# The last six token tiles as three units of 1024 tokens, the first FFN product by Strassen's seven products, with weight sums built on the chip and streamed back from DRAM

## The chip, the cores and the metric

The kernel runs on one core of one Trainium2 chip. The metric is the time of one execution in microseconds of device time; a run's figure is the median of several executions. The program is written in Bass with a hand-written order: the text of the program is the order of instructions on each engine. TensorE (PE) multiplies, VectorE (DVE), ScalarE (ACT) and GpSimd (POOL) work elementwise, and SyncE (SP) issues the transfers.

## What is computed

The reference, cut to what matters. Attention is local: each block of 64 tokens attends only to itself.

```python
def _attn_ref(q, k, v):                       # B, H, S, D = 8, 8, 576, 64
    ...
    scores = scale * np.matmul(q_c, k_c.transpose(0, 1, 2, 4, 3))     # chunks of 64
    scores = scores - np.max(scores, axis=-1, keepdims=True)
    attn = np.exp(scores)
    attn = attn / (np.sum(attn, axis=-1, keepdims=True) + 1e-09)
    out = np.matmul(attn, v_c)
    ...
def _moe_ref(x, g_ln, w_ch1, w_ch2):          # 4608 tokens, 512 -> 2048 -> 512
    ...
    xn = (x - mu) / np.sqrt(var + 1e-06) * g_ln
    ch = np.maximum(xn @ w_ch1, 0.0) @ w_ch2
    return (x + ch).astype(np.float32)
```

## The kernel before, in words

The 4608 tokens are 9 tiles of 512 (`NTILE`), each tile two pairs of 256 (`PAIR`, 18 pairs). Every matmul operand of the FFN is held as a high and a low part, and a product is the sum of three matmuls: high by high, high by low, low by high. The hidden width 2048 is cut into 16 slices `f` of 128.

Per tile, `ffn` runs over the 16 slices. `up(f)` (L427) makes the hidden slice `h`, 128 by 512 tokens, in one PSUM bank: 4 slices of the width 512 by 3 terms, 12 matmuls at L437. `split(f)` rectifies it on ACT into the high part `hh` (L447) and leaves the remainder `hl` on DVE (L448). `down(f)` (L453) adds 12 matmuls (4 token blocks by 3 terms, L458) into the four PSUM banks `y`. `finish` (L471) scales `y` by the reciprocal root of the variance, adds `x` and stores. So a tile has 192 matmuls of 128x512 in the first product and 192 in the second. PSUM has 8 banks: 2 for attention (`ps_a`), 2 for `h` (`ps_h`), 4 for `y` (`ps_y`).

`attention` is a generator; each `next` on it issues one step for one pair: loads; scores (L243, 64 small matmuls); row maxima `top`; subtraction and exponential; 16 transposes of 32x256 on DVE (L298); row sums; the product with V into two `ps_h` banks (L327); scaling to `x`; statistics (L371); `xg` (L376); 16 more transposes of 32x256 on DVE (L410) and the split into `xth` (ACT, L415) and `xtl` (POOL, L416). With `by_pe` the transposes are done on TensorE instead, into `ps_a` banks, and copied out by ACT.

All weights stay in SBUF as `wp[f]` once they are converted from the float64 words that come from DRAM (`convert_w`). The strings `START`, `STEADY` and `LAST` are the order: each letter advances one generator (`u` the FFN matmuls, `1` split or finish, capital letters attention). `START` covers tile 0 and the weight conversion. `STEADY` is played for tiles 1 to 7 and carries two pairs of attention for the tiles behind; `LAST` is tile 8 alone. SP issues every transfer but a few in program order; an issue that waits for something holds those behind it.

Of the kernel before, what the change touches and what calls it, by code (L numbers as in the profile page):

```python
# [8 lines left out]
F32 = mybir.dt.float32  # L9
# [8 lines left out]
P = 128  # L18
# [16 lines left out]
START = "kkwkwakwbkwkwkawwwwaawwbwabbkwAkwawbwakkabkkaabaAbabauw1Abbub1Bkbwvuuwuw12wwAvvvw22AwvwvuAvw2wwAvvw1u2AuwwBwvuv12vBuuwyywABA1ww3Ayww3wAywAyuwwwwA3y3BywBBBwBEyyBBwy3w3yywBwwyww3BwwyByy3ywy33yy3E"  # L35
STEADY = "ABu1Au1AuAu1AuAu1AuABuAu1AEu1AuAu1AuAu1AuAu1BuBu1BuBu1BuBu1BuBEuBBu1BBu1BuBBu1Buu1uu1"
LAST = "u1u1uu1uu1uu1uu1uu1uu1uu1uu1uu1uu1uu1uu1uu1uu1u1"

# [7 lines left out]

ROOM = (3, 11)

F64_LOW = float.fromhex("0x1p-15")
F64_HIGH = float.fromhex("0x1.dffffep+16")  # L50


# [5 lines left out]
def chunk_attention_ffn(ctx: ExitStack, tc: tile.TileContext, qkv, v01, g, w, out):  # L58
# [12 lines left out]
    ps_h = ctx.enter_context(tc.tile_pool(name="ps_h", bufs=2, space=PSUM))  # L71
    ps_y = ctx.enter_context(tc.tile_pool(name="ps_y", bufs=4, space=PSUM))

    ident = const.tile([P, P], F32, name="ident")
# [130 lines left out]

    def attention(pair, xt_cols, xs, by_pe, den_by_pe):

# [161 lines left out]
        for j in range(2):  # L369
            stats = small.tile([P, nc.vector.BN_STATS_DIM], F32, name="stats")  # L370
            nc.vector.bn_stats(out=stats, in_=x[:, j, :])  # L371
            nc.vector.bn_aggr(out=mv[:, j, :], in_=stats)
        yield
        xg = work.tile([P, 2, DM], F32, name="xg", tag="work")
        for j in range(2):
            nc.vector.scalar_tensor_tensor(  # L376
                out=xg[:, j, :], in0=x[:, j, :], scalar=mv[:, j, 0:1], in1=g_sb, op0=ALU.subtract, op1=ALU.mult
            )
        yield

        xth, xtl = xt_cols()
# [38 lines left out]
    def ffn(pairs, xt, xs, f0, f1, room=()):  # L420
# [3 lines left out]
        hs, held = {}, []  # L424
        tail = pairs[-1] == 2 * NTILE - 1

# [16 lines left out]
        def split(f):  # L443
            if slots == 1 or not held:
                held[:] = [hp_.tile([P, slots, nt], F32R, name=f"h{i}") for i in "hl"]
            h, (hh, hl) = hs[f], (x[:, f % slots, :] for x in held)
            nc.scalar.activation(hh, h, AF.Relu)  # L447
            nc.vector.scalar_tensor_tensor(  # L448
                out=hl, in0=h, scalar=0.0, in1=hh.bitcast(F32), op0=ALU.max, op1=ALU.subtract
            )  # L450
            hs[f] = hh, hl
# [19 lines left out]
        def finish(j):  # L471
            pair, jj = pairs[j // 2], j % 2
            x, rstd = xs[pair]
            nc.vector.scalar_tensor_tensor(  # L474
                out=x[:, jj, :], in0=sums(pair)[jj], scalar=rstd[:, jj : jj + 1], in1=x[:, jj, :],
# [31 lines left out]
        def rectified():  # L507
            for f in range(f0, f1):
                assert f < f0 + 2 or f - 2 in done
                split(f)  # L510
# [9 lines left out]

        return products(), rectified()

    def play(order, streams):
        for c in order:
            next(streams[c])
# [3 lines left out]
    class Tokens:  # L529
# [10 lines left out]
        def attention(self, i, by_pe=False, den_by_pe=False):  # L540
            return attention(2 * self.t + i, lambda: self.cols(i), xs, by_pe, den_by_pe)

# [13 lines left out]
    with tc.manual_schedule():  # L556
        nc.scalar.activation(minus, ident, AF.Copy, scale=-1.0)
        play(START, now)
        for t in range(1, NTILE):
            now.update(zip("u1", tiles[t].ffn(0, 2, room=ROOM if t + 1 < NTILE else ())))  # L560
            if t + 1 < NTILE:
                now.update(A=now.pop("E"), B=tiles[t + 1].attention(1))
            now["E"] = tiles[t + 2].attention(0) if t + 2 < NTILE else iter("  ")
            play(STEADY if t + 1 < NTILE else LAST, now)

# [34 lines left out]
```

## Time and profile before

| what | value |
|---|---|
| time, median of 3 runs | 864.1 us (863.63 to 864.87) |
| span of the profiled execution, first to last instruction | 862.8 us |
| tile 1 starts on PE | 131.7 us |
| one period of two tiles in `STEADY` | 183.1 us (247.57 to 430.66) |
| bytes moved in the whole execution | 60.39 MB, mean 70 GB/s |

The profile is one execution taken by the hardware profiler; the median of the timed runs lies 1.3 us above its span. A matmul's listed duration contains the pipeline; how far apart matmuls start is what counts for a full PE. The busy share of an engine is a mean over stages that have different limits, so the stages are read one by one.

### The profile page before, as it was taken

What the parts mean: (1) busy time and instruction counts of PE and PEld (TensorE: products, weight loads), DVE (VectorE), ACT (ScalarE), POOL (GpSimd) and SP (SyncE); (2) the same over time, 40 slices, a digit from 0 to 9 for tenths busy, and PEclk for the clock granted to TensorE, in tenths of its full rate; (3) what the DMA queues carried; (4) which work ended last, traced back from release to release, by engine and by line L of the source; (5) the groups of instructions that cost most, each with busy time, mean ns of one, the idle gap of its engine ahead of it and who ended that gap; (6) DMA issues with size and microseconds to landing.
All of it is one profiled execution on the core that took longest, in us unless ns stands there. A gap on an engine that the chain in (4) does not pass through costs nothing.

```text
span 862.8 us, 13752 instructions
## 1 busy us (share of the span) xinstructions
PE 852.4 (99%) x5946; PEld 704.5 (82%) x5946; DVE 526.1 (61%) x960; ACT 178.6 (21%) x267; POOL 56.7 (7%) x64
## 2 busy tenths in 40 slices
PE   7999999999999999999999999999999999999998
PEld 5888888888888888888888888888888888888886
DVE  6989957567556665666657575676566656661112
ACT  5766431021112121201111111211120212011110
POOL 0110000010101010101000100101010101010000
PEclk9999999999999999999999999999999999999999
DMA  9996503200320032001310032003200300010001
GB/s 356 331 291 182 195 1 123 74 1 2 122 74 1 1 111 86 1 1 39 112 47 2 1 122 74 1 2 122 75 1 2 121 27 1 1 49 0 1 1 49
DMA packets 19499, 60.39 MB, mean 70 GB/s; under 512 B 2160, under 2 KB 2160, under 8 KB 17520
## 3 DMA queue, kind: packets, MB, share of 16 engines
q1 hardware_dynamic: 18144, 54.81, 17.7%
q0 software_dynamic: 1296, 4.72, 2.8%
q8 instruction: 46, 0.75, 0.4%
q14 instruction: 13, 0.11, 0.0%
HBM read 45.37 MB, written 9.44 MB: 64 GB/s over the span
## 4 chain that ended last, share of the span: by engine, by line
PE 94%; DVE 3%; DMA 2%; issue 0%; SPq 0%; ACT 0%; DVEq 0%
PE y L458 45%; PE h L437 44%; PE s L243 2%; PE h L327 2%; DMA wp<-wfs 1%; DMA k_t<-qkv 1%; PE s L269 0%; DVE xg L376 0%; DVE wfs L132 0%; DVE stats L371 0%; DVE top L250 0%; DVE wfs L139 0%; PE s L327 0%; PE s L390 0%; DVE wfs L129 0%
## 5 line engine op out<-in xcount | busy, mean ns | idle before, releaser
L437 PE MATMUL h<-xth,wp 128*128 128x512 f32 (+1 forms) x1200 | 377.4, 381 | 1.0 <-DMA wp<-wfs 1.0
L458 PE MATMUL y<-wp,hh 128*128 128x512 f32 x1152 | 289.0, 391 | 0.0
L448 DVE SCALAR_TENSOR_TENSOR hl<-h,hh 128x512 fp32r<-128x512 f32 (+1 forms) x150 | 100.1, 670 | 270.2 <-ACT hh L447 265.0
L437 PEld LDWEIGHTS h<-xth,wp 128*128 128x128 f32 x1200 | 222.4, 188 | 45.4 <-DMA wp<-wfs 1.2
L458 PEld LDWEIGHTS y<-wp,hh 128*128 128x128 f32 x1152 | 214.5, 188 | 44.5
L437 PE MATMUL h<-xtl,wp 128*128 128x512 f32 (+1 forms) x600 | 227.5, 381 | 0.0
L447 ACT ACTIVATE hh<-h 128x512 fp32r<-128x512 f32 (+1 forms) x150 | 86.5, 579 | 563.2 <-PE h L437 544.4
L458 PE MATMUL y<-wp,hl 128*128 128x512 f32 x576 | 156.0, 389 | 0.0
L437 PEld LDWEIGHTS h<-xtl,wp 128*128 128x128 f32 x600 | 112.4, 188 | 21.7 <-ACT xtl L400 0.2
L458 PEld LDWEIGHTS y<-wp,hl 128*128 128x128 f32 x576 | 108.2, 188 | 22.6
L410 DVE STREAM_TRANSPOSE xt<-xg 32x256 f32<-32x256 f32 x224 | 97.6, 436 | 3.7
L298 DVE STREAM_TRANSPOSE pt_sb<-p_sb 32x256 f32<-32x256 f32 x224 | 97.6, 436 | 3.1
L416 POOL TENSOR_TENSOR xtl<-xt,xth 128x512 fp32r<-128x512 f32 x28 | 35.6, 1292 | 587.0 <-ACT xth L415 587.0
L474 DVE SCALAR_TENSOR_TENSOR x<-y,rstd,x 128x512 f32<-128x512 f32 x36 | 24.8, 746 | 28.9 <-PE y L458 28.1
L361 DVE TENSOR_TENSOR x<-h,rden 128x512 f32<-128x512 f32 x28 | 18.0, 686 | 12.1 <-PE h L327 12.1
L376 DVE SCALAR_TENSOR_TENSOR xg<-x,mv,g_sb 128x512 f32<-128x512 f32 x36 | 25.3, 744 | 0.0
L371 DVE BATCH_NORM_STATS2 stats<-x 128x6 f32<-128x512 f32 x36 | 24.3, 675 | 0.2
L276 ACT ACTIVATE p_sb<-p_sb 128x1024 f32<-128x1024 f32 x16 | 17.0, 1060 | 35.8 <-DVE p_sb L275 35.8
L250 DVE TENSOR_REDUCE top<-s 128x16 f32<-128x1024 f32 x18 | 21.9, 1216 | 1.2 <-PE s L243 1.2
L415 ACT CAST xth<-xt 128x512 fp32r<-128x512 f32 x28 | 16.0, 618 | 31.5 <-DVE xt L410 31.5
L468 POOL TENSOR_TENSOR rstd<-vare,mhalf 128x2 f32<-128x2 f32 x18 | 12.1, 692 | 141.5 <-DVE vare L466 141.5
L243 PE MATMUL s<-k_t,q_t 64*64 64x64 f32 x1088 | 19.1, 219 | 1.0 <-DMA k_t<-qkv 0.7
(83 smaller groups left out, 311.1 us busy)
## 6 DMA issues: line engine op xcount, KB each, us to landing
raw<-w SPq DMA_DIRECT2D x15, 1024.0 KB, 7.5
out<-x SPq DMA_DIRECT2D x36, 256.0 KB, 2.2
q_t<-qkv SPq DMA_DIRECT2D x17, 512.0 KB, 4.8
k_t<-qkv SPq DMA_DIRECT2D x17, 512.0 KB, 5.7
v_t<-qkv SPq DMA_DIRECT2D x32, 256.0 KB, 4.2
wp<-wfs POOLq DMA_DIRECT2D x6, 512.0 KB, 6.4
wp<-wf POOLq DMA_DIRECT2D x3, 512.0 KB, 8.1
v<-v SPq DMA_DIRECT2D x4, 260.0 KB, 10.9
```

The costliest lines, as they stand in the source:

```text
L243: nc.tensor.matmul(s[h2][c * D : (c + 1) * D, j * HP + a, :], lhsT=q_t[r, a, cs], rhs=k_t[r, a, cs], start=not den_by_pe or j == a == 0, s ...
L250: nc.vector.tensor_reduce(out=top, in_=s4, axis=AX.X, op=ALU.max)
L298: nc.vector.transpose(out=pt_sb[quad(2 * h2 + j), :, c, quad(i)], in_=p_sb[quad(2 * c + i), :, h2, quad(j)])
L371: nc.vector.bn_stats(out=stats, in_=x[:, j, :])
L376: nc.vector.scalar_tensor_tensor(out=xg[:, j, :], in0=x[:, j, :], scalar=mv[:, j, 0:1], in1=g_sb, op0=ALU.subtract, op1=ALU.mult)
L410: nc.vector.transpose(out=xt[quad(j), :, quad(i)], in_=xg[quad(i), :, quad(j)])
L416: nc.gpsimd.tensor_tensor(out=xtl[:, :, js], in0=xt_j, in1=xth[:, :, js].bitcast(F32), op=ALU.subtract)
L437: nc.tensor.matmul(h, lhsT=(wh, wh, wl)[m][:, ks], rhs=(xth, xtl, xth)[m][:, k, :], start=i == 0, stop=i == len(terms) - 1,)
L447: nc.scalar.activation(hh, h, AF.Relu)
L448: nc.vector.scalar_tensor_tensor(out=hl, in0=h, scalar=0.0, in1=hh.bitcast(F32), op0=ALU.max, op1=ALU.subtract)
L458: nc.tensor.matmul(sums(pairs[j // 2])[j % 2], lhsT=(hh, hh, hl)[m], rhs=(wh, wl, wh)[m], start=f == 0 and m == 0, stop=f == NF - 1 and m ...
L474: nc.vector.scalar_tensor_tensor(out=x[:, jj, :], in0=sums(pair)[jj], scalar=rstd[:, jj : jj + 1], in1=x[:, jj, :], op0=ALU.mult, op1=ALU.add,
```

## The change

Tiles 0, 1 and 2 keep the old FFN (`LEAD = 3`); tiles 3 to 8 become three units of two tiles, 1024 tokens each (`unit_ffn`). `START` is the same on every engine.

**First product.** Two slices of the hidden width by two tiles, with the width 512 halved, is a 2x2 by 2x2 block product. Strassen's scheme (in Winograd's form) needs 7 block products in place of 8. One block product is 2 x 3 = 6 matmuls of 128x512 (`product`), so two slices for two tiles take 42 matmuls in place of 48, a unit 336 in place of 384. Sums of blocks go through PSUM where they can (products accumulate onto banks that still hold another product); snapshots of a bank are copied to SBUF by ACT (32 per unit, L810 to L838) and 24 sums per unit are made by DVE (`add`, L775) into `hu`, which holds the whole hidden layer of the unit. The second product has 384 matmuls as before (L853), and its operands are split from `hu` in SBUF.

**Weight sums.** During tiles 1 and 2 `prepare` forms the sums of weight blocks on POOL, splits them into high and low on ACT and POOL, and writes them to DRAM scratch (`wa`, 14.7 MB; the second weights `w2d`, 8.4 MB). From then on each unit streams 60 blocks of 512 KB back through a ring of 6 places (28 of `wa`, and the 16 of `w2d` twice), one block per 12 matmuls.

**Token sums.** `combine` makes the sums of token blocks on DVE (`less`, 5 per half unit) and splits seven operands per half on ACT and POOL (`part`).

**Attention** of tiles 3 to 8 ends in `rows` in place of `xth`/`xtl`: the variance's root now multiplies `xg` on ACT (L438), the 16 last transposes of 32x256 become 32 of 32x128, and the split moves to `combine`. Three pairs (both of tile 4, the first of tile 3) do their transposes on TensorE. `x` of every pair from tile 2 on is written to DRAM and read back for the final addition.

**Order.** `SECOND` and `THIRD` replace `STEADY` for tiles 1 and 2. In units, `weave` issues attention steps at fixed counts of matmuls (`STEPS`, a pair every 138); units 0 and 1 carry the four pairs of the unit behind, unit 2 carries nothing. The core of the diff:

```diff
+def prepare():                      # per pair of slices, 8 times, four steps each
+    for i in range(2):
+        nc.gpsimd.tensor_tensor(out=t_[:, i], in0=both[i][:, 0, :DM]..., in1=both[i][:, 1, :DM]..., op=ALU.add)
+        nc.sync.dma_start(w2d[fe + i], both[i][:, :, DM:].bitcast(F32))
+    yield
+    nc.gpsimd.tensor_tensor(...)    # four of 128x256
+    for to, of in late:
+        nc.sync.dma_start(to, of.bitcast(F32))
+    nc.sync.dma_start(wa[q][:, e, 0], ...)      # three of these
+    yield
+    r = raws.tile([P, 2, 2, 2, PAIR], F32R, name="parts", tag="raw")
+    nc.scalar.copy(r[:, 0], t_)
+    yield
+    nc.gpsimd.tensor_tensor(out=r[:, 1], in0=t_, in1=r[:, 0].bitcast(F32), op=ALU.subtract)
+    late = [...]                    # four stores of r, issued in the next round
+    yield
...
+def unit_ffn(u):
...
+    for q in range(NF // 4):
+        banks = [ps_y.tile([P, DM], F32, name="y") for _ in range(4)]
+        c_, a_ = banks[0::2], banks[1::2]
+        for e in range(2):
+            w0, w1 = pair_of()
+            product(c_[e], w0, "2", True)
+            yield 6
+            product(a_[e], w1, "1", True)
+            ring.fetch()
+            nc.scalar.copy(s[e][0], a_[e])
+            add(h[e][:, 0, 0], c_[e], s[e][0])
+            yield 6
+        for e in range(2):
+            product(a_[e], w0, "6", False)
+            nc.scalar.copy(s[e][1], a_[e])
+            yield 6
+            product(c_[e], w1, "5", True)
+            nc.scalar.copy(s[e][2], c_[e])
+            yield 6
+        for e in range(2):
+            product(a_[e], w0, "7", False)
+            add(h[e][:, 1, 1], a_[e], s[e][2])
+            yield 6
+            product(c_[e], w1, "3", False)
+            add(h[e][:, 1, 0], c_[e], s[e][1])
+            yield 6
+        for e in range(2):
+            product(a_[e], w01[e], "4", False)
+            nc.scalar.copy(h[e][:, 0, 1], a_[e])
+            yield 6
...
-for t in range(1, NTILE):
-    ...
-    play(STEADY if t + 1 < NTILE else LAST, now)
+play(layout(ROOMS[1], SECOND), now)
+play(layout(ROOMS[2], THIRD, True), now)
+for u in range(UNITS):
+    ...
+    weave(unit_ffn(u), side)
```

What stands on PE in `STEADY` before: the end of one slice's second product (`hh`, `hl`), the value product (L327) and the next pair's scores (L243) side by side, and the next slice.

```order
L458 MATMUL y<-wp,hh 128x512 x8
L458 MATMUL y<-wp,hl 128x512 x4
L327 MATMUL h<-v_t,pt_sb 64x64 x32
L243 MATMUL s<-k_t,q_t 64x64 x32
L458 MATMUL y<-wp,hh 128x512 x8
L458 MATMUL y<-wp,hl 128x512 x4
```

On PE in the first product of units 0 and 1, from the unit's first matmul (`xc` are the token operands, `ring` the streamed weights; L294 are scores, L378 value products):

```order
L769 MATMUL y<-xc,ring 128x512 x12
L294 MATMUL s<-k_t,q_t 64x64 x32
L769 MATMUL y<-xc,ring 128x512 x78
L378 MATMUL h<-v_t,pt_sb 64x64 x32
L769 MATMUL y<-xc,ring 128x512 x60
L294 MATMUL s<-k_t,q_t 64x64 x32
L769 MATMUL y<-xc,ring 128x512 x78
L378 MATMUL h<-v_t,pt_sb 64x64 x32
L769 MATMUL y<-xc,ring 128x512 x60
L294 MATMUL s<-k_t,q_t 64x64 x32
L769 MATMUL y<-xc,ring 128x512 x48
```

The large matmuls are 336 (12 + 78 + 60 + 78 + 60 + 48), and scores and value products, which stood together, now stand apart.

On DVE before, at the end of a pair's attention in `STEADY` (L448 is the remainder `hl` of a hidden slice, which PE waits for):

```order
L448 SCALAR_TENSOR_TENSOR hl_3554<-h_3540,hh_3553 128x512
L376 SCALAR_TENSOR_TENSOR xg_3557<-x_3530,mv_3533,g_sb_96 128x512 x2
L410 STREAM_TRANSPOSE xt_3560<-xg_3557 32x8x32 x4
L448 SCALAR_TENSOR_TENSOR hl_3579<-h_3565,hh_3578 128x512
L410 STREAM_TRANSPOSE xt_3560<-xg_3557 32x8x32 x12
L448 SCALAR_TENSOR_TENSOR hl_3620<-h_3606,hh_3619 128x512
L448 SCALAR_TENSOR_TENSOR hl_3653<-h_3639,hh_3652 128x512
```

On DVE in unit 0, at the end of the first pair's attention, in the second of the four rounds `q` of the first product (`hu<-y,snap` are the sums that give PSUM banks free; `top` and `p_sb` already belong to the second pair):

```order
L434 SCALAR_TENSOR_TENSOR xg_3680<-x_3642,mv_3660,g_sb_98 128x512 x2
L457 STREAM_TRANSPOSE rows_2519<-xg_3680 32x4x32 x8
L775 TENSOR_TENSOR hu_3397<-y_3590,snap_3403 128x512
L457 STREAM_TRANSPOSE rows_2519<-xg_3680 32x4x32 x8
L775 TENSOR_TENSOR hu_3397<-y_3589,snap_3403 128x512
L457 STREAM_TRANSPOSE rows_2519<-xg_3680 32x4x32 x8
L775 TENSOR_TENSOR hu_3398<-y_3592,snap_3404 128x512
L775 TENSOR_TENSOR hu_3398<-y_3591,snap_3404 128x512
L457 STREAM_TRANSPOSE rows_2519<-xg_3680 32x4x32 x8
L301 TENSOR_REDUCE top_3807<-s_3754 128x16
L326 TENSOR_TENSOR p_sb_3820<-s_3754,top_3807 128x2x8x64
L775 TENSOR_TENSOR hu_3399<-y_3831,snap_3403 128x512
```

Four waits of PE on DVE (the `hu` sums) now stand among the transposes, one behind each eight of them.

On ACT before, around the exponential (L276), only rectifications (L447) and splits (L415):

```order
L447 ACTIVATE hh_3280<-h_3267 128x512
L415 CAST xth_3223<-xt_3225 128x4x128 x2
L447 ACTIVATE hh_3317<-h_3304 128x512
L276 ACTIVATE p_sb_3339<-p_sb_3339 128x1024
L447 ACTIVATE hh_3355<-h_3342 128x512
```

On ACT in unit 0, at the same place as the DVE rows (snapshots L810 to L820, the copies of the round's last products L838, the exponential L327):

```order
L820 COPY snap_3403<-y_3589 128x512
L816 COPY snap_3404<-y_3592 128x512
L820 COPY snap_3404<-y_3591 128x512
L838 COPY hu_3397<-y_3590 128x512
L327 ACTIVATE p_sb_3820<-p_sb_3820 128x1024
L838 COPY hu_3398<-y_3592 128x512
L810 COPY snap_3403<-y_3832 128x512
L810 COPY snap_3403<-y_3834 128x512
```

The copy that frees the bank `y_3592`, and the first snapshots of the next round, stand behind the second pair's exponential.

More of the change, by code (lines that the diff above doesn't have):

```diff
@@ L424, in ffn @@
         hs, held = {}, []
[L425 removed]
+        tail = pairs[-1] == 2 * LEAD - 1
         def up(f):
@@ L443, in split @@
         def split(f):
-            if slots == 1 or not held:
+            if tail and f == NF - 1:
+                last = raws.tile([P, 2, 1, nt], F32R, name="last", tag="raw")
+                held[:] = [last[:, i] for i in range(2)]
+            elif slots == 1 or not held:
                 held[:] = [hp_.tile([P, slots, nt], F32R, name=f"h{i}") for i in "hl"]
@@ L523, in play, with weave @@
+    def weave(ffn, side):
+        at = 0
+        side = sorted(side, key=lambda x: x[0])
+        for cost in ffn:
+            at += cost
+            while side and side[0][0] <= at:
+                next(side.pop(0)[1])
+        assert not side
     def play(order, streams):
```

329 lines of the change are left out of this document (319 added, 10 removed), and 3 rows, old and new, of the table SECOND.

## The prediction

> **What bounds the kernel now.** I read the page's busy shares and chain first, then the stages, then the chain in order of time.
>
> ```profile
> PE 852.4 (99%) x5946; PEld 704.5 (82%) x5946; DVE 526.1 (61%) x960; ACT 178.6 (21%) x267; POOL 56.7 (7%) x64
> PE 94%; DVE 3%; DMA 2%; issue 0%; SPq 0%; ACT 0%; DVEq 0%
> 0.00:131.60 131.60, 125.05 (x1146) 102.49 (x1146) 106.12 (x153) 72.01 (x97) 10.38 (x20) 1.00 0.68 223
> 223.40:772.50 549.10, 549.10 (x3781) 454.84 (x3780) 347.44 (x674) 83.16 (x132) 38.59 (x36) 1.00 0.13 45
> 247.57 5.44 PE h L437 x24
> 850.78 8.21 PE y L458 x36
> ```
>
> PE is 94% of the chain. In the second stage row (tiles 2 to 7, columns: length, then PE, PEld, DVE, ACT, POOL busy, granted clock, DMA share, GB/s) it has no idle time at all, at a granted clock of 1.00, while DVE is busy 347.44 of 549.10 (63%) and DMA 0.13. So time there is the number of matmuls times their pitch: 24 in 5.44 us, 0.2267 us each (36 in 8.21 in the tail agree). Whatever removes matmuls is gained one for one, as long as PE stays full. The first stage row, tile 0 and the weights, is not touched.
>
> **What PE gains and pays.** Each unit has 336 large matmuls in its first product where two tiles had 384: 48 x 3 = 144 fewer, 144 x 0.2267 = **32.6 us less**. The second product and tiles 1 and 2 keep theirs.
>
> Next, the small products that interrupt the large ones. PE's order of time, with the two kinds side by side and with one alone:
>
> ```profile
> 239.72 1.98 PE L458 MATMUL y<-wp,hh 128*128 128x512 f32 x8
> ...
> 242.53 1.16 PE L327 MATMUL h<-v_t,pt_sb 64*64 64x64 f32 x64
> 243.51 1.11 PE L243 MATMUL s<-k_t,q_t 64*64 64x64 f32 x64
> ...
> 247.41 0.39 PE L437 MATMUL h<-xth,wp 128*128 128x512 f32 x1
> ```
>
> ```profile
> 127.81 1.98 PE L458 MATMUL y<-wp,hh 128*128 128x512 f32 x8
> ...
> 130.62 1.16 PE L243 MATMUL s<-k_t,q_t 64*64 64x64 f32 x64
> 131.71 0.50 PE L437 MATMUL h<-xth,wp 128*128 128x512 f32 x1
> 132.05 0.39 PE L437 MATMUL h<-xtl,wp 128*128 128x512 f32 x1
> ```
>
> Between 239.72 and 247.41 stand 24 large matmuls (5.44): both kinds together cost 7.69 - 5.44 = 2.25 us. From 127.81, 12 large ones end at 130.53; the second matmul behind the scores starts at 132.05, one pitch after 131.82: one kind alone costs 1.29. From tile 1 on, before has 13 couples and one single, 30.5 us; the change has 3 couples and 21 singles, 33.8. **3.3 us more.** Three pairs also get transposes on PE: three batches of eight (`p_sb`) and six of four (`xg`).
>
> ```profile
> 75.09 0.60 PE L390 MATMUL s<-ident,xg 128*128 128x128 f32 x4
> 75.45 2.10 PE L458 MATMUL y<-wp,hh 128*128 128x512 f32 x8
> 77.39 1.08 PE L458 MATMUL y<-wp,hl 128*128 128x512 f32 x4
> ...
> 88.77 1.03 PE L287 MATMUL s<-ident,p_sb 128*128 128x128 f32 x8
> 89.56 2.09 PE L458 MATMUL y<-wp,hh 128*128 128x512 f32 x8
> 91.49 1.08 PE L458 MATMUL y<-wp,hl 128*128 128x512 f32 x4
> ```
>
> A batch of four: from 75.09 to 77.39 less eight pitches, 0.49. A batch of eight: 88.77 to 91.49 less eight pitches, 0.91. 6 x 0.49 + 3 x 0.91 = **5.7 us more**. So a PE that never waits would take 862.8 - 32.6 + 3.3 + 5.7 = 839.2 us of span. That span stands 1.3 below the median, so 840.5. This is a floor, and the rest is what PE waits.
>
> **Waits on DVE and ACT in the first product of units 0 and 1.** Per unit DVE had 63% of 183 us, 115 us. It gets 24 sums and 10 `less` of 128x512 (0.69 each, 23 us) and, in four pairs, 32 small transposes in place of 16. Their cost is not in the trace. Bounds are half of the 32x256 transpose and all of it, 0.22 and 0.44. I take 0.30: with half the columns L448 falls by 0.273 for 256 elements, so 128 fewer take 0.137 off 0.436. That is 4 x (9.6 - 7.0) = 10 us. DVE comes to 148 of some 173 us, 86%. What matters is the order within it.
>
> ```profile
> L448 DVE SCALAR_TENSOR_TENSOR hl<-h,hh 128x512 fp32r<-128x512 f32 x138 | 95.4, 691 | 270.2 <-ACT hh L447 265.0 <-PE y L458 4.2
> L410 DVE STREAM_TRANSPOSE xt<-xg 32x256 f32<-32x256 f32 x224 | 97.6, 436 | 3.7
> L376 DVE SCALAR_TENSOR_TENSOR xg<-x,mv,g_sb 128x512 f32<-128x512 f32 x36 | 25.3, 744 | 0.0
> L371 DVE BATCH_NORM_STATS2 stats<-x 128x6 f32<-128x512 f32 x36 | 24.3, 675 | 0.2
> L372 DVE BATCH_NORM_AGGREGATE mv<-stats 128x2 f32<-128x6 f32 x36 | 6.6, 182 | 1.2
> L250 DVE TENSOR_REDUCE top<-s 128x16 f32<-128x1024 f32 x18 | 21.9, 1216 | 1.2 <-PE s L243 1.2
> L276 ACT ACTIVATE p_sb<-p_sb 128x1024 f32<-128x1024 f32 x16 | 17.0, 1060 | 35.8 <-DVE p_sb L275 35.8
> L415 ACT CAST xth<-xt 128x512 fp32r<-128x512 f32 x28 | 16.0, 618 | 31.5 <-DVE xt L410 31.5
> L416 POOL TENSOR_TENSOR xtl<-xt,xth 128x512 fp32r<-128x512 f32 x28 | 35.6, 1292 | 587.0 <-ACT xth L415 587.0
> L448 DVE SCALAR_TENSOR_TENSOR hl<-h,hh 128x256 fp32r<-128x256 f32 x12 | 4.7, 418 | 0.1
> ```
>
> Take the second round of a unit and start the clock when product 1 of its second slice is done. DVE: the snapshot (0.6), a sum (0.7), statistics (2 x 0.86), `xg` (1.5), ACT's new scaling of `xg` (0.6), then three times eight transposes and a sum (3 x 3.1): the sum that frees the last bank ends at 14.4. PE needs that bank after nine products of 1.36 and one batch of scores, at 13.5: 0.9 late. Then DVE has another sum, eight transposes, `top` and the subtraction (about 1.2 each), to 19.9, and ACT the exponential (1.06) and, queued behind it, the copy of that bank, 21.6. PE wants the bank again at 13.5 + 0.9 + four products = 19.9: 1.7 late. The last round, where 32 small transposes and `top` stand between the sums of its two halves, costs about 1 by the same count. So 3.6 per unit, **7.2 us** in units 0 and 1; unit 2 carries no attention and pays nothing. With transposes at 0.22 all of it vanishes; at 0.44 the three places give 4.2, 2.8 and 5, 24 us for two units. In the second product operands are split three groups of 12 ahead, 8 us, which hides the 0.6 and 0.7 of each.
>
> **Tiles 1 and 2.** POOL does the weight sums: by L416, two of 1.29, four of some 0.65 and one of 2.6 per pair of slices, 7.8 us, against about five groups of 2.72 in the order, 13.6. ACT's cast waits for them and for the four stores of the round before; behind it stand the rectifications, which PE needs 5.4 us after it made `h`, some 4 us more than 0.6 and 0.7. I count that as hidden; without cover each microsecond is paid eight times. In tile 2 one place has no work between: transposes of `xg` and, in the same PSUM tile, the next pair's transposes, which wait for ACT's copy (0.6 and the way there), 1 us, and at two or three other places a PSUM tile comes back about as late as PE wants it. I take **2 us** for the stage, 0 to 8.
>
> **Transfers.** One unit moves 60 blocks of 0.524 MB, 31.5, and for four pairs q, k, v, `x` out, `x` back and the result, 12.6: 44 MB in 173 + 4 us, 250 GB/s, five times what the stage moves now.
>
> ```profile
> q_t<-qkv SPq DMA_DIRECT2D x17, 512.0 KB, 4.8
> 0.00:21.57 21.57, 17.03 (x209) 11.14 (x213) 13.66 (x18) 11.07 (x15) 0.86 (x8) 1.00 0.92 356
> 43.14:64.71 21.57, 20.58 (x244) 17.96 (x243) 18.80 (x27) 14.62 (x21) 3.48 (x4) 1.00 0.99 291
> ```
>
> The start moves 356 GB/s, and 291 in its worst full slice, so 250 fits. A block is asked for five groups, 13.6 us, before it is used; one of its size lands in 4.8. On SP a request stands behind loads of a pair (1.5 MB, 4 us) and behind the store of `x`, which waits for DVE. I cost it at nothing; the price if it isn't hidden is a rival.
>
> **The sum:** 862.8 - 32.6 + 3.3 + 5.7 + 7.2 + 2 = 848.4 of span, **849.7 us** as a time; bounds of the unknown costs 840.5 and 840.5 + 24 + 8 = 872.
>
> **The rivals.**
> 1. PE never waits: **840.5**. For it: DVE's 86% leaves room, and operations overlap a little. Against it: the count above puts two sums behind their need. 0.20.
> 2. DVE is the bound of the first product: small transposes near 0.44, about 24 + 2 us of waits, **866**; halfway, 857. For it: 24 of them between sums. Against it: the measured slope of L448. 0.20 for 856 and above, 0.03 of it near 864, within 0.2% of no change.
> 3. DVE and POOL stand in each other's way. In units the remainders read two SBUF operands instead of one from PSUM, while POOL makes 14 subtractions of 1.29 per unit: if each holds DVE up for its length, 18 us per unit, for which DVE has some 25 free; it lags by more than its lead now and then, say 4 us per unit, **857**. Nothing in the trace speaks for it:
>
> ```profile
> 267.80 2.54 POOL L416 TENSOR_TENSOR xtl<-xt,xth 128x512 fp32r<-128x512 f32 x2 [46.77 <-ACT xth L415]
> 270.06 0.69 DVE L448 SCALAR_TENSOR_TENSOR hl<-h,hh 128x512 fp32r<-128x512 f32 x1 [2.99 <-ACT hh L447]
> ```
>
> While POOL subtracts here, DVE is idle (2.99 us before 270.06), so the two do not meet in these rows. Chance 0.05. [...]
> 4. The stream does not keep up, and the change is **slower**. The place is the ring in units 0 and 1: PE waits for weights. Against 849.7 it takes 14.4 us more, 7.2 per unit, to lose all: 44 MB in 184 us, 239 GB/s. Below that rate of mixed reads and writes it decides; at 220 a unit takes 200 us, **+46, 896**. For it: before writes only 9.4 MB, so no row shows the mix. Against it: 356 and 291 with one queue. 0.08.
>
> **Chances.** Forecast (845 to 856) 0.47, then 0.20, 0.20, 0.05, 0.08. Faster by over 0.2% (1.7 us, about what a measurement can tell from no change) is 0.47 + 0.20 + 0.17 + 0.05 = 0.89, within it 0.03, slower 0.08. The range, 840 to 862, leaves out the stream and the worst of DVE.
>
> **What would show it.** PE's busy time should fall by some 24 us and its idle time grow from 10 to about 19, put down to DVE `hu` sums and ACT copies in the second and last rounds of units 0 and 1; unit 2's first product should be 336 x 0.2267 = 76.2 us without a gap. Waits of PE on `ring` would show rival 4, `STREAM_TRANSPOSE rows` far from 300 ns rival 1 or 2, remainders much above 691 ns rival 3. Wrong altogether I am if the pitch itself changes, 0.2267 with streamed operands.

## The result, and the profile after

The changed kernel takes **879.2 us** (median of 4 executions, 875.69 to 880.14) against 863.9 (863.63 to 864.87) for the kernel before: a ratio of 1.0168, 95% interval 1.0147 to 1.0188. It is **slower by 1.7%**, where 849.7 was forecast and 840 to 862 given as the range. The fastest of the four, 875.69, had a mean granted clock of 0.996, the other three 0.990 to 0.992: what the clock does differs from execution to execution, and a profile is one execution.

The page of the changed kernel: busy times with their share of the span, the chain's shares, one group of instructions, and one row of the transfers (columns: size, us from issue to landing).

```profile
span 878.3 us, 14775 instructions
PE 843.6 (96%) x5850; PEld 686.8 (78%) x5850; DVE 569.8 (65%) x1101; ACT 270.3 (31%) x425; POOL 150.0 (17%) x138
PE 75%; DVE 14%; issue 6%; DMA 2%; ACT 2%; POOL 1%; SPq 0%; ACTq 0%; POOLq 0%; DVEq 0%
L457 DVE STREAM_TRANSPOSE rows<-xg 32x128 f32<-32x128 f32 x288 | 71.6, 282 | 4.1 <-ACT xg L438 2.0
ring<-wa SPq DMA_DIRECT2D x84, 512.0 KB, 4.3
```

PE's share of the chain fell from 94% to 75%, and DVE's rose from 3% to 14%: PE now waits. Its busy time fell from 852.4 to 843.6 us. The stages show where (columns: length, busy PE, PEld, DVE, ACT, POOL, granted clock, DMA share, GB/s). The rows are tiles 1 and 2, unit 0, unit 1 and unit 2:

```profile
131.60:341.30 209.70, 198.08 (x1553) 162.44 (x1546) 130.99 (x244) 52.77 (x82) 86.75 (x78) 0.98 0.59 204
341.30:525.50 184.20, 178.51 (x1234) 144.03 (x1233) 144.72 (x321) 53.98 (x92) 26.28 (x20) 0.99 0.70 232
525.50:709.70 184.20, 178.47 (x1234) 144.04 (x1233) 144.07 (x320) 53.00 (x90) 23.52 (x18) 0.99 0.71 235
709.70:874.60 164.90, 164.87 (x721) 134.90 (x719) 43.56 (x64) 38.47 (x64) 0.00 (x0) 1.00 0.64 207
```

Set against a PE that never waits (the prediction's floor, cut at the same places: 193.0, 173.5, 173.5 and 163.2), the stages lose 16.3, 10.7, 10.7 and 1.6 us (the first counted from tile 1's first matmul at 131.99 to unit 0's at 341.21). That is the difference between the floor of 839.2 and the span of 878.3, within rounding. PE's waits in unit 0 (columns: total us, times, longest) and then in tiles 1 and 2:

```profile
PE h L378 <- DVE pt_sb L349: 3.6, 2, 3.1
PE y L769 <- ACT hu L838: 1.0, 1, 1.0
PE y L853 <- ACT hx L788: 0.7, 1, 0.7
PE y L769 <- DVE hu L775: 0.4, 1, 0.4
```

```profile
PE s L338 <- ACT p_sb L327: 3.9, 2, 2.4
PE s L448 <- DVE p_sb L326: 3.1, 1, 3.1
PE h L378 <- DVE hl L533: 2.3, 1, 2.3
PE s L378 <- ACT pt_sb L340: 1.5, 1, 1.5
PE s L338 <- ACT rows L449: 0.8, 1, 0.8
```

No row names `ring`: the weight stream keeps up. The largest wait in unit 0 stands in the **second** product, where the prediction had none. It is the fourth pair's value product, waiting for transposed probabilities. The rows around it in order of time:

```profile
459.87 1.22 DVE L326 TENSOR_TENSOR p_sb<-s,top 128x1024 f32<-128x1024 f32 x1
461.13 1.06 ACT L327 ACTIVATE p_sb<-p_sb 128x1024 f32<-128x1024 f32 x1 [8.85 <-DVE p_sb L326]
462.09 1.66 ACT L788 ACTIVATE hx<-hu 128x512 fp32r<-128x512 f32 x3
462.75 5.86 PE L853 MATMUL y<-ring,hx 128*128 128x512 f32 x24 [0.71 <-ACT hx L788]
...
470.91 1.81 DVE L349 STREAM_TRANSPOSE pt_sb<-p_sb 32x256 f32<-32x256 f32 x4
471.94 0.30 PE L378 MATMUL h<-v_t,pt_sb 64*64 64x64 f32 x2 [3.07 <-DVE pt_sb L349]
```

ACT stands idle 8.85 us in front of an exponential whose input DVE has not made yet, and three rectifications that could have run are queued behind it. DVE in turn is late with the transposes. Behind the wait the granted clock halves (columns: length, PE busy, clock, DMA share, GB/s):

```profile
469.83:473.24 3.41, 0.76 (x32) 1.00 0.37 144
473.24:476.66 3.42, 3.42 (x48) 0.50 0.02 5
```

There are four such halves in this execution before PE's last matmul: two in tile 2, one each in units 0 and 1.

### The profile page after: what moved, and what is told of

It reads as the page before. It is cut to its first block, busy times and chain, and to the rows that moved or that the text cites. A ratio compares the mean times of both kernels' runs of the same rounds, so it can differ in the third digit from the quotient of the medians.

```text
span 878.3 us, 14775 instructions
## 1 busy us (share of the span) xinstructions
PE 843.6 (96%) x5850; PEld 686.8 (78%) x5850; DVE 569.8 (65%) x1101; ACT 270.3 (31%) x425; POOL 150.0 (17%) x138
## 4 chain that ended last, share of the span: by engine, by line
PE 75%; DVE 14%; issue 6%; DMA 2%; ACT 2%; POOL 1%; SPq 0%; ACTq 0%; POOLq 0%; DVEq 0%
PE y L769 22%; PE y L853 19%; PE y L543 11%; PE h L519 11%; PE h L853 8%; DVE rows L457 3%; DVE pt_sb L349 2%; PE s L294 1%; PE h L378 1%; DMA wp<-wfs 1%; DVE xg L434 1%; DVE p_sb L326 1%; DVE hu L775 1%; DVE stats L422 1%; DVE xt L492 1%
## 5 line engine op out<-in xcount | busy, mean ns | idle before, releaser
L769 PE MATMUL y<-xc,ring 128*128 128x512 f32 x1008 | 233.2, 391 | 2.7 <-ACT hu L838 2.0
L769 PEld LDWEIGHTS y<-xc,ring 128*128 128x128 f32 x1008 | 188.1, 188 | 43.9 <-ACT hu L838 2.8
L853 PE MATMUL y<-ring,hx 128*128 128x512 f32 x486 | 132.6, 400 | 1.5 <-ACT hx L788 1.5
L519 PE MATMUL h<-xth,wp 128*128 128x512 f32 (+1 forms) x432 | 130.1, 372 | 1.3 <-DMA wp<-wfs 1.3
L853 PEld LDWEIGHTS y<-ring,hx 128*128 128x128 f32 x486 | 91.6, 190 | 24.0 <-ACT hx L788 2.3
L775 DVE TENSOR_TENSOR hu<-y,snap 128x512 f32<-128x512 f32 x72 | 48.8, 688 | 82.9 <-ACT snap L810 50.8
L543 PE MATMUL y<-wp,hh 128*128 128x512 f32 x376 | 96.3, 394 | 0.0
L519 PEld LDWEIGHTS h<-xth,wp 128*128 128x128 f32 x432 | 79.0, 190 | 16.1 <-DMA wp<-wfs 1.5
L543 PEld LDWEIGHTS y<-wp,hh 128*128 128x128 f32 x376 | 69.4, 189 | 14.0
L519 PE MATMUL h<-xtl,wp 128*128 128x512 f32 (+1 forms) x216 | 78.8, 369 | 0.0
L853 PE MATMUL y<-ring,hh 128*128 128x512 f32 x252 | 71.8, 395 | 0.0
L853 PEld LDWEIGHTS y<-ring,hh 128*128 128x128 f32 x252 | 47.7, 190 | 11.2 <-DVE hu L775 0.6
L543 PE MATMUL y<-wp,hl 128*128 128x512 f32 x188 | 51.8, 389 | 0.0
L853 PE MATMUL h<-ring,hx 128*128 128x512 f32 x162 | 50.9, 395 | 0.0
```

Of the source, the lines that this page charges most:

```text
L519: nc.tensor.matmul(h, lhsT=(wh, wh, wl)[m][:, ks], rhs=(xth, xtl, xth)[m][:, k, :], start=i == 0, stop=i == len(terms) - 1,)
L543: nc.tensor.matmul(sums(pairs[j // 2])[j % 2], lhsT=(hh, hh, hl)[m], rhs=(wh, wl, wh)[m], start=f == 0 and m == 0, stop=f == NF - 1 and m ...
L769: nc.tensor.matmul(bank, lhsT=w[:, (0, 0, 1)[m], ks], rhs=x[:, (0, 1, 0)[m], k, :], start=start and k == m == 0, stop=k == 1 and m == 2, s ...
L775: nc.vector.tensor_tensor(out=out, in0=bank, in1=s, op=ALU.add)
L853: nc.tensor.matmul(ys[j], lhsT=(hh, hh, hl)[m], rhs=w[:, (0, 1, 0)[m]], start=f == 0 and m == 0, stop=f == NF - 1 and m == 2,)
```

## The experiments

Four theories were set against each other. **A**: ScalarE's queue order, as above. **B**: VectorE is behind by the sum of its work, whoever is queued. **C**: VectorE and GpSimd hold each other up. **D**: idle time of PE halves its clock, which costs on its own. Lengths of stages below run from the first matmul of one unit to that of the next (of unit 2, to its own last matmul), in each run's trace. "By the distance of starts" means the time from one matmul's start to the next one's, less the first one's pitch. Where an expectation names 879, it is the changed kernel.

### ScalarE's instructions behind their producers

```diff
-STEPS = (0, 8, 16, 30, 40, 50, 60, 70, 80, 87, 95, 105, 116, 126, 136, 146)
+STEPS = (0, 8, 16, 24, 30, 40, 50, 60, 70, 80, 87, 95, 105, 112, 116, 126, 136, 146)
 nc.vector.tensor_tensor(out=p_b, in0=s4, in1=top4, op=ALU.subtract)
+if pair >= 2 * LEAD + 4:
+    yield
 nc.scalar.activation(p_sb, p_sb, AF.Exp, scale=scale)
```

The two scalings of `xg` (L438) get a step of their own in the same way.

> Of the attention steps that lie beside units 0 and 1, the exponential is issued 8 matmuls behind its subtraction instead of with it, and the two scalings of the normalized rows 7 matmuls behind the rows, so that ScalarE's rectifications are no longer queued behind an instruction that waits for VectorE. Theory A (ScalarE's queue order is what loses the time in units 0 and 1): the 0.87 us wait for hx at 461.66 and the ones behind it go, the half clock at 473 and 657 with them, and units 0 and 1 fall from 184.2 us to 175 to 178 each: 863 to 868 us. Theory B (VectorE is behind by the sum of its work, whoever is queued): the wait of the fourth pair's value product for the transposed probabilities stays at 3 to 4 us, units at 182 to 185, 876 to 880 us. Theory C (VectorE and GpSimd hold each other up): as theory B.

Measured 873.2 us (872.78 to 874.82), ratio 1.0096 (1.0070 to 1.0123). Units 0 and 1 take 181.4 us, 2.8 less each. PE's waits in unit 0:

```profile
PE h L380 <- DVE pt_sb L351: 2.4, 2, 1.9
PE y L775 <- DVE hu L781: 0.9, 2, 0.5
```

The waits for ACT (`hx`, `hu`) are gone, the wait for the transposes fell from 3.6 to 2.4 us, and the half clock stays. A is a part of the cause, a quarter of the units' loss, and not the whole.

### The value product 12 matmuls later

```diff
-STEPS = (0, 8, 16, 30, 40, 50, 60, 70, 80, 87, 95, 105, 116, 126, 136, 146)
+STEPS = (0, 8, 16, 30, 40, 50, 60, 70, 92, 98, 104, 110, 116, 126, 136, 146)
```

> Beside units 0 and 1 each pair's value product is issued 12 matmuls (2.7 us) later, and what follows it up to the rows is drawn together; nothing else changes. Theory B (PE waits at the fourth pair because VectorE is behind by the sum of its work): the wait of 3.3 + 0.7 us for the transposed probabilities shrinks by 2.7 to about 1.3 us, the half clock behind it (3.4 us at half speed, some 1.7 us) does not come, and units 0 and 1 fall by 4 to 5 us each: 869 to 871 us. If PE's wait is set by ScalarE's queue (theory A), or the lost time turns up in a later wait for an operand, they fall by under 2 us: 875 to 879 us.

Measured 870.7 us (869.88 to 871.72), ratio 1.0075 (1.0059 to 1.0092), inside what B gave; units at 180.6, no half clock in them.

```profile
PE y L769 <- DVE hu L775: 1.7, 1, 1.7
PE y L853 <- DVE hl L789: 1.2, 1, 1.2
PE y L769 <- ACT hu L838: 1.0, 1, 1.0
```

The wait for the transposes is gone altogether, and 1.2 us turn up as a wait for `hl`. A remainder that is issued three groups (8 us) ahead now comes late, so DVE's queue is itself that far behind: B.

### The first combinations behind the fourth value product

```diff
-ONE_STEP = 8
-FIRST_HALF = 345
+ONE_STEP = 7
+FIRST_HALF = 512
```

> The first half's combinations (4 subtractions of 0.69 us on VectorE, 7 copies of 0.57 us on ScalarE, 7 subtractions on GpSimd) are issued from matmul 512 of units 0 and 1 instead of 345, behind the fourth pair's value product. Theory B: VectorE is 2.8 us less behind there, so the wait of 4.0 us falls to about 1.3, the half clock does not come, and the wait of 0.9 us for hx goes too: units fall by 4 to 6 us each, 867 to 871 us. If it is not the sum of VectorE's work that makes PE wait, or if the combinations now delay the second half's operands: 876 to 882 us.

Measured 873.7 us (872.64 to 874.96), ratio 1.0111 (1.0094 to 1.0127); units at 181.9 and 180.8, no half clock in them. The time lies above B's 867 to 871. The wait for the transposes fell to 0.5 us, as B has it, but in unit 0 2.2 us of waits for `hl` and `hx` came 23 to 36 us later, where the combinations now stand. So work taken from DVE ahead of the wait shortens it as B says, and it has to be paid where it is put.

### GpSimd quiet in the units

Left out: the low halves of the seven operands of units 1 and 2, which stay those of unit 0.

```diff
-nc.gpsimd.tensor_tensor(out=o[:, 1, :, cs], in0=x, in1=o[:, 0, :, cs].bitcast(F32), op=ALU.subtract)
+if not quiet:
+    nc.gpsimd.tensor_tensor(out=o[:, 1, :, cs], in0=x, in1=o[:, 0, :, cs].bitcast(F32), op=ALU.subtract)
...
-stream = combine(half)
+stream = combine(half, True)             # True is quiet
```

> The low halves of the seven operands of units 1 and 2 are left out (they stay those of unit 0), so that GpSimd does nothing of the combinations beside units 0 and 1. Theory C (VectorE and GpSimd hold each other up): remainders there take 691 ns, none of them 0.98 to 1.36 us, VectorE is about 2 us less behind in front of the fourth pair, and units 0 and 1 fall by 2 to 6 us each (the half clock at 473 and 657 may go too): 867 to 875 us. Theories A (ScalarE's queue order) and B (the sum of VectorE's work): units stay within 1 us of 184.2, 877 to 880 us.

Measured 879.3 us (877.75 to 879.74), ratio 1.0160 (1.0134 to 1.0187): no gain in time. The remainders from 420 to 520 us, of the changed kernel and then of this one:

```profile
L789 DVE SCALAR_TENSOR_TENSOR hx<-hu,hx 128x512 fp32r<-128x512 f32 x18 | 14.8, 840 | 6.2 <-ACT hx L788 6.0
```

```profile
L790 DVE SCALAR_TENSOR_TENSOR hx<-hu,hx 128x512 fp32r<-128x512 f32 x18 | 12.2, 690 | 7.8 <-ACT hx L789 6.0 <-PE h L854 1.6
```

C is real: with GpSimd quiet each takes 690 ns instead of 840, and DVE's busy time in the unit falls from 144.7 to 139.9 us. PE's wait for the transposes stays at 3.5 us and the units at 184.1, but not because nothing was gained. The wait of 0.7 us for `hx` is gone, and the fourth pair's value product starts 126.4 us behind the unit's first matmul instead of 127.3. In return this execution has two windows at half clock in a row in each unit, where the changed kernel's had one. The `hx` row and the first of the two windows here:

```profile
461.30 5.82 PE L854 MATMUL y<-ring,hx 128*128 128x512 f32 x24
469.66:473.07 3.41, 2.24 (x60) 0.50 0.05 18
```

So C costs about 0.9 us in each unit ahead of that wait, and the extra window hides the gain. What such a second window costs shows in the run with the weight sums spread over tile 1, whose unit 0 has the changed kernel's order: it too has two of them and takes 184.8 us instead of 184.2. The forecast of C, 2 to 6 us a unit, was too large all the same.

### The weight sums spread over tile 1

```diff
-    0: "CDS", 1: "CDS", 2: "DGS", 3: "CS", 4: "CDDS", 5: "DS", 6: "DS", 7: "DG", ...
+    0: "CD", 1: "CD", 2: "DG", 3: "C", 4: "CDD", 5: "D", 6: "D", 7: "DG", ...
```

The seven letters `S` go into the seven entries of `SECOND` that had none.

> The seven steps of the weight sums that lay beside tile 2 are spread over tile 1, so that GpSimd and ScalarE do nothing of them in tile 2. Theory C (VectorE and GpSimd hold each other up): the small sum that took 2.2 us at 220.9 and the normalized rows that took 4.06 us instead of 1.40 at 233.1 go back to theirs, the PE wait of 3.3 us at 236.8 falls under 1, and the half clock at 241 goes: tile 2 loses 16.3 - 5 = 11 us instead of 16.3, 873 to 875 us, if tile 1 takes the denser steps without a wait. If the order on VectorE alone is what PE waits for in tile 2: 878 to 880 us. Denser steps that cost tile 1 waits of their own would show there, up to 4 us.

Measured 874.9 us (873.61 to 875.27), ratio 1.0110 (1.0078 to 1.0141). Unit 0 starts 5.9 us earlier, at 335.3. Of that, 1.8 us come from tile 0, which the edit does not touch (tile 1's first matmul stands at 130.22 instead of 131.99). From that matmul to unit 0 it is 205.1 us instead of 209.2. The place in the changed kernel, and then in this one:

```profile
232.48 2.39 POOL L648 TENSOR_TENSOR parts<-sums,parts 128x1024 fp32r<-128x1024 f32 x1
233.07 4.06 DVE L434 SCALAR_TENSOR_TENSOR xg<-x,mv,g_sb 128x512 f32<-128x512 f32 x2
240.37 0.63 PE L448 MATMUL s<-ident,xg 128*128 128x128 f32 x4 [3.13 <-DVE p_sb L326]
```

```profile
231.31 1.40 DVE L434 SCALAR_TENSOR_TENSOR xg<-x,mv,g_sb 128x512 f32<-128x512 f32 x2
235.99 0.63 PE L448 MATMUL s<-ident,xg 128*128 128x128 f32 x4 [0.52 <-DVE p_sb L326]
```

Here C is on the path. `xg` takes 4.06 us beside GpSimd's subtraction, 1.40 without it, 2.66 less. The wait goes from 3.13 to 0.52 us, 2.61 less, and the half clock behind it does not come; the two make the 4.1 us.

### Tile 2 in another order, on top of it

```diff
-ROOMS = {1: (3, 11), 2: (6,)}
+ROOMS = {1: (3, 11), 2: (7,)}
-    ..., 12: "GP", 13: "GHP", 14: "GHP", 15: "GGP", 16: "GGHP", 17: "GGP", 18: "P", 19: "HHP", 20: "HP", ...
+    ..., 12: "GP", 13: "P", 14: "P", 15: "GHP", 16: "GHP", 17: "HGGP", 18: "GGP", 19: "GGP", 20: "HHP", ...
```

> The weight sums as in the run that spread them over tile 1 (874.9 us), and in tile 2 the value product of the third tile's second pair one f later, and the last pair's subtraction and exponential ahead of the other pair's 32 small transposes instead of between them, its value product two steps later. If the waits of 2.5, 2.6 and 1.7 us at 270, 292 and 298 come from what is queued ahead on VectorE, they go, with the half clock at 274: 874.9 - 2.5 - 1.7 - 2.6 - 1.7 = 866.4 us, 866 to 869. If they are only handed on to the next step of the same pairs: 872 to 876 us.

Measured 872.0 us (871.11 to 873.72), ratio 1.0097 (1.0077 to 1.0116); unit 0 starts at 331.6, and from tile 1's first matmul it is 199.9 us, 5.2 less than in the run before. The waits of 2.3 and 2.4 us are gone, and tile 2's last half clock with them. But the last value product (L378) now waits 2.9 instead of 1.5 us: it was handed on in part.

### The place of the hx tiles

```diff
+pad = small.tile([P, 48], F32, name="pad", bufs=1)       # ahead of the pool with hx: 192 bytes; in two more runs 16 and 32 elements
...
+nc.gpsimd.memset(pad, 0.0)
```

> One unused tile of 192 bytes a partition ahead of the pool that holds the hx tiles: they begin 192 bytes later, at the same remainder of 512 bytes as the hh and hl tiles; nothing else changes. If the pitch of 231 and 236 ns of the second product's matmuls with hx as the stationary operand (227 ns with hh and hl) comes from where the tile begins, all of them come at 226 to 227 ns, unit 2 falls from 164.9 to 163.2 us, and 216 matmuls by 6.8 ns in each of three units make 4.4 us: 874 to 875 us. If it comes from the pool's region or from the writes into it, 233.5 ns in the mean stay, and 879 us.

> As the run with 192 bytes ahead of the hx tiles, with 64: they begin at remainder 32 of 128 bytes as the hh and hl tiles do, but at another remainder of 256 and 512 bytes. If the slow pitch is a matter of 128 bytes, the matmuls with hx come at 227 ns, if of 256 or 512 bytes, at 231 and 236 ns.

> As the run with 192 bytes ahead of the hx tiles, with 128: they begin at remainder 96 of 128 bytes, as in the changed kernel, and in the lower half of 256 and 512 bytes (remainder 96) instead of the upper one. If the slow pitch is a matter of 128 bytes, 231 and 236 ns stay; if of 256 or 512 bytes, 227 ns.

With 192 bytes the run took 877.0 us (872.66 to 878.83), ratio 1.0129 (1.0092 to 1.0167), not 874 to 875: its trace has six windows at half clock before PE's last matmul, the changed kernel's four. Unit 2, which has none in either, takes 163.0 us instead of 164.6. One execution with 64 bytes took 879.3 us, one with 128 bytes 874.2. PE's order of time in unit 2 has 36 matmuls with `hx` and then `hh`; the distance of the two starts is 36 pitches. The rows of the changed kernel, of 192, of 64 and of 128 bytes:

```profile
791.18 8.56 PE L853 MATMUL y<-ring,hx 128*128 128x512 f32 x36
799.58 2.00 PE L853 MATMUL y<-ring,hh 128*128 128x512 f32 x8
```

```profile
791.53 8.32 PE L855 MATMUL y<-ring,hx 128*128 128x512 f32 x36
799.69 1.98 PE L855 MATMUL y<-ring,hh 128*128 128x512 f32 x8
```

```profile
790.65 8.53 PE L855 MATMUL y<-ring,hx 128*128 128x512 f32 x36
799.01 1.98 PE L855 MATMUL y<-ring,hh 128*128 128x512 f32 x8
```

```profile
786.42 8.40 PE L855 MATMUL y<-ring,hx 128*128 128x512 f32 x36
794.66 1.98 PE L855 MATMUL y<-ring,hh 128*128 128x512 f32 x8
```

That is 8.40 / 36 = 233.3 ns, then 226.7, 232.2 and 228.9. Nothing differs but where the tiles begin (remainders of 512 bytes: 480, 160, 32, 96; `hh`, `hl` and the ring begin at 160), so in these four traces the pitch goes with the place. A matter of 128 bytes it is not, since 64 bytes should then have been fast. A matter of the half of 512 bytes it is not either: 32, 96 and 160 lie in the lower half and give 232.2, 228.9 and 226.7. The runs with 64 and 128 bytes are one execution each, and why the pitch differs was not shown.

The run with 128 bytes shows something else. Its order in tiles 1 and 2 is the changed kernel's, and so are PE's waits there, each to within 0.1 us. Yet none of them sets off a half clock. Its largest wait, and the two windows in which it lies:

```profile
239.27 0.63 PE L450 MATMUL s<-ident,xg 128*128 128x128 f32 x4 [3.16 <-DVE p_sb L328]
233.93:237.34 3.41, 2.18 (x10) 1.00 0.98 255
237.34:240.76 3.42, 1.49 (x9) 1.00 1.01 395
```

In the changed kernel's trace the same wait lay mostly in one window, 237.73 to 241.14, in which PE was busy for 0.78 us, and the next window was at half clock. So of two waits of 3.1 and 3.2 us the one that lay in one window was followed by a half clock, and the one that was split, with 2.18 and 1.49 us busy, was not. From tile 1's first matmul to unit 0 the same order takes 206.0 us here with no half clock, 209.2 in the changed kernel with two, and 210.4 in the run with 64 bytes with three. That is 1.6 us each for the first two, and more than half of the 5.9 us between the spans of the two traces (878.3 and 872.4).

### Useless matmuls in the wait

```diff
+if pair in (13, 17):                       # the fourth pairs of the tokens of units 1 and 2
+    wide = minus.rearrange("p (one n) -> p one n", one=1).broadcast_to([P, NK, P])
+    for i in range(8):                     # in the second run 16
+        nc.tensor.matmul(o[i % 2], lhsT=minus, rhs=wide, start=True, stop=True)
 for j in range(2):
```

> In front of the fourth pair's value product of units 0 and 1 PE does eight 128x512 matmuls more, without use, into the bank that the value product then fills anew: 8 x 0.227 = 1.8 us of work in a wait of 4.0 us. The wait ends when VectorE's transposes end, so that is not moved. Theory D (the clock record's halves of 3.41 us follow a window of the same length in which PE did nothing for some 1.9 us or more, and cost by themselves): no half clock at 473 and 657, and each of the two units falls by 1.5 to 2 us though PE has 1.8 us more to do: 875 to 876.5 us. If the half clock is not set off by the idle time, or costs nothing since PE waits there anyway: 879 us or more, up to 883 if the eight matmuls lengthen the units.

> As the run with eight useless matmuls in front of the fourth pair's value product of units 0 and 1, with sixteen: 16 x 0.227 = 3.6 us of the wait of 4.0 us, which ends when VectorE's transposes end. Eight left 1.35 + 0.80 us of idle time, and the half clock still came behind it. Theory D (a window of 3.41 us with some 1.9 us or more of PE idle, small matmuls counting little, halves the next window): now under 1.2 us are left idle, no half clock comes at 473 and 657, and each of the two units falls by 1 to 2 us though PE has 3.6 us more to do: 875 to 877.5 us. If the half clock is not set off by the idle time: it stays, 879 us. If the matmuls are not hidden in the wait: 881 to 886 us.

Pairs 13 and 17 are those whose attention runs beside units 0 and 1.

With eight: 879.5 us (878.50 to 880.17), ratio 1.0165 (1.0141 to 1.0189). With sixteen: 876.3 us (874.70 to 877.73), ratio 1.0125 (1.0096 to 1.0154), and units 0 and 1 at 182.7 us, 1.5 less each, with 3.6 us more of work. The two windows around the wait, with eight and with sixteen (columns as above):

```profile
470.20:473.60 3.40, 1.65 (x55) 0.99 0.35 136
473.60:477.00 3.40, 3.40 (x33) 0.50 0.03 5
```

```profile
469.83:473.24 3.41, 3.38 (x20) 1.00 0.49 161
473.24:476.66 3.42, 3.20 (x67) 1.00 0.00 0
```

With eight, D's forecast of 875 to 876.5 failed: they ran from 468.56 to about 470.4, most of them in the window before, and left waits of 1.35 and 0.80 us in this one. With 1.65 us busy of 3.40 the clock still halves; with 3.38 it does not, though the work behind waits for the same transposes. So here the half clock came and went with the idle time of the window, and one half clock cost 1.5 us in each of these two units: D. The intervals of the two ratios, with sixteen and of the changed kernel, just overlap; the reading rests on the windows of the traces.

### All of it together

The edits of the runs above without the quiet GpSimd and the useless matmuls, the value product 8 matmuls later instead of 12.

> All of it together: exponential and scalings issued behind their producers, hx tiles moved by 192 bytes, weight sums in tile 1, the new order of tile 2, the value product 8 matmuls later, the first combinations behind matmul 512. If the losses add up as the traces split them (tile 2: 6.0 + 8.5, units 10.7 each, pitch 1.6 a unit, less what is left of the waits in the first products, 0.6 to 1.7 a unit): 879.2 - 14.5 - 2 x 9 - 4.4 = 842 us, 842 to 850 us, faster than before. If one loss hides behind another: 852 to 860 us.

Measured **852.9 us** (852.17 to 854.63), ratio 0.9872 (0.9854 to 0.9890): faster than the kernel before, though not the 842 to 850 that were expected if the losses add up. The stages from tile 1 on:

```profile
131.60:330.75 199.15, 193.50 (x1520) 158.59 (x1519) 126.61 (x242) 53.23 (x82) 85.08 (x76) 1.00 0.61 213
330.75:506.90 176.15, 174.63 (x1233) 142.50 (x1232) 145.86 (x321) 54.30 (x92) 26.33 (x20) 1.00 0.71 242
506.90:683.30 176.40, 174.82 (x1234) 142.55 (x1233) 145.39 (x320) 53.27 (x90) 23.77 (x18) 1.00 0.71 245
683.30:846.60 163.30, 163.30 (x721) 134.96 (x719) 43.53 (x64) 38.48 (x64) 0.00 (x0) 1.00 0.62 209
```

The arithmetic and the streams are those of the changed kernel, and the clock is full in every row. So most of what the changed kernel loses is in the placing of steps and of one pool: of 39 us, 28 are back (span 850.4). The rest is waits, some 6 us around tile 2 and 2.8 in each of the two units. The full clock is in part luck: a wait of 3.0 us at 297.8 lies astride two windows, with 1.6 and 2.4 us busy. Another of the run's four executions had a mean clock of 0.996 and took 854.63 us.

A last order for tile 2 on top of it, with the last steps of its second pair one step earlier, both halves of the first rows' transposes in one step, and the last value product one step later:

```diff
-24: "BCS", 25: "BBS", 26: "BS", 27: "BBS", 28: "BBS"
+24: "BBCS", 25: "BBS", 26: "BBS", 27: "BBS", 28: "S"
-3: "C", 4: "CDD", ... 22: "HP", 23: "HH"
+3: "CC", 4: "DD", ... 22: "P", 23: "H", 24: "HH"
```

> As the run with all parts together (852.9 us), with four waits of tile 2 taken on by order alone: the last steps of tile 2's second pair one step earlier in tile 1 (the wait of 1.6 us at 217), both halves of the first rows' transposes in one step (0.7 and 1.0 us at 236 and 240), the last value product one step later (3.0 us at 298). If they are waits for an order on VectorE and ScalarE: 3 to 6 us less, 847 to 850 us. If they are handed on to the next steps: 851 to 854 us.

Measured 851.9 us (851.53 to 852.18), ratio 0.9849 (0.9830 to 0.9868). The medians differ by 1.0 us, but unit 0 starts where it did, at 330.75, and the profiled span is the same 850.4. The wait of 2.9 us for the last value product is gone, and two smaller ones stand in its place: handed on.

## Why the prediction was wrong, point by point

- **The gain in matmuls was right.** Unit 2's first product, 336 matmuls without attention beside it, takes 76.2 us as said. So was the cost of the small transposes (0.30 estimated, 282 ns measured), and rival 4 fell: no wait on `ring`, 4.3 us from issue to landing at 232 GB/s. PE's busy time did not show the gain: it fell by 8.8 us and not by some 24, and its idle time is 34.7 us and not about 19, in part because time at half clock (473.24 to 476.66: 3.42 us busy at 0.50) and at a slower pitch (233.3 ns with `hx`) counts as busy.
- **Waits in the first product, 3.6 us per unit: too large.** By the distance of starts, the two places in the second round cost 0.55 and 1.15 us (0.9 and 1.7 forecast), and the last round costs nothing. The mechanism is the one that was counted. (The combinations have 4 subtractions on DVE per half unit, 8 per unit, not the 5 and 10 that were counted: 1.4 us of its work.)
- **The step that failed in the units** is "In the second product operands are split three groups of 12 ahead, 8 us, which hides the 0.6 and 0.7 of each". It compared the lead with the length of a split and not with how far DVE's queue is behind, and it put the waits of this stage at nothing. The largest wait there, for the transposed probabilities of the fourth pair, is an attention step for which the sum has no term at all. DVE has the attention, the remainders and the combinations there at once. The runs with a later value product and later combinations show the lag, the one with ScalarE's instructions set back shows ACT's queue, which the sum did not follow in this stage. The three waits there (0.87, 3.27 and 0.74 by the distance of starts) are 4.9 us per unit, the half clock they set off 1.5, the pitch 1.6, and small gaps make the rest of 9.0.
- **Tiles 1 and 2, "2 us, 0 to 8": 16.3.** Tile 1 lost nothing up to its last slice (1.6 us); the rest is tile 2's. The one place that was named (transposes behind transposes in one PSUM tile) costs the 1 us that was said. "Two or three other places" where something comes "about as late as PE wants it" were passed over without a count; by the distance of starts they are five waits of 1.6 to 3.3 us, 12.6 us with that 1 us, and the two half clocks, 3.2 us in the comparison above, make nearly all of the rest.
- **Rival 3, VectorE and GpSimd, 0.05:** the mechanism is there, remainders at 840 ns against 690. In the units, where it was placed, it costs about 0.9 us each instead of 4, and it sets the largest wait of tile 2, where the weight sums run. So its price was too high where it was looked for, and its larger place was not looked at.
- **Two terms were missing.** A window in which waits left PE idle for 2.15 us (1.35 and 0.80, with eight useless matmuls) was followed by 3.40 us at a clock of 0.50, and the sum priced a wait at its length alone. And the pitch: "wrong altogether I am if the pitch itself changes" came true in part. It is 0.2267 in unit 2's first product (76.2 us for 336), with streamed operands, but 0.233 with `hx` as the stationary operand, 1.6 us per unit.
- **The sum again with what was measured:** 848.4 - 2 x 1.9 (first products) + 2 x 9.0 (10.7 - 1.7, nearly all of it in the second products) + 14.3 (tile 2) + 1.6 (unit 2) = 878.5, beside 878.3. The rival for slower put the loss in the transfers; it came from the order of steps on DVE and ACT.

## What to carry to other kernels

When a change empties PE's queue of work, count for every engine how far its whole queue is behind at each place that PE waits for, in the stage where most side work overlaps; a lead in issue order hides a producer's length, not its engine's backlog (a remainder issued 8 us ahead came 1.2 us late). An instruction that waits for another engine, put ahead of ready ones in program order, holds them up (ACT stood idle for 8.85 us with three rectifications behind an exponential): issue it a step behind its producer, which gave 2.8 us in each of two units here. A loss that comes only from placing is worth an experiment before the change is given up: here the same arithmetic went from 1.7% slower to 1.5% faster. And before a difference of a few microseconds between two traces is put down to an edit, count the windows at half clock in both: two of them were 3.2 of 5.9 us here.

## What was not expected of the hardware

- **The clock's windows.** In these traces the half clocks lie on a grid of 3.41 us whose place differs from trace to trace: in the changed kernel they begin at 241.14, 278.68, 473.24 and 657.56, which are 11, 57 and 54 times 3.413 us apart, and with eight useless matmuls one begins at 473.60. In the changed kernel, from tile 1 to PE's last matmul, the four windows ahead of a half clock have PE busy for 0.78, 1.12, 0.76 and 0.89 us of 3.41, and the least busy of the windows at full clock that are followed by another, 299.16 to 302.57, for 1.68. In the 14 traces of the changed kernel and the experiments, from tile 1 on and cut on that grid, 39 windows at full clock are followed by one at half clock. With PE's idle time counted by the distance of starts, each of these 39 has at least 2.0 us of it, and of the windows at full clock that are not followed by one none has more than 2.1. That is a count of these traces; behind a window that is itself at half clock no such border was found.
- **The pitch was not the same at four places of the stationary tile:** 226.7, 228.9, 232.2 and 233.3 ns for the same matmuls, with `hx` beginning at 160, 96, 32 and 480 bytes within 512. Each is 36 matmuls of one trace.
- **VectorE beside GpSimd.** Two `xg` took 4.06 us from 233.07 on in the changed kernel, beside a GpSimd subtraction of 2.39 us from 232.48 and the sums behind it, and 1.40 us with the weight sums in tile 1. Remainders took 840 ns with GpSimd's subtractions in the unit and 690 without. Which operands matter was not varied.
